# Inverse roots and two tiles' inverse sums as GpSimd powers in a linear-attention block

## The chip, the cores and the metric

One core of one Trainium2 chip. The metric is device time in microseconds of one execution of the whole program, as a median over runs.

In the profile PE is TensorE (PEld its weight loads), DVE is VectorE, ACT is ScalarE, POOL is GpSimd, and SP is the engine that issues nearly all DMAs. Each engine works through its own queue in order; a semaphore wait holds the instruction that has it and everything behind it on that engine.

## The reference

The block has 2048 tokens of width 576, 32 heads of 18 features, and an MLP of width 4608. Cut to what matters:

```python
mod = silu(c) @ w_mod                        # sa, ca, ga, sb, cb, gb
h = layernorm(x) * (1 + ca) + sa             # norm 1, 1 / sqrt(var + eps)
q, k, v = split(h @ wqkv)
phi_q = concat(softmax(q @ w_phi), softmax(-q @ w_phi))
phi_k = concat(softmax(k @ w_phi), softmax(-k @ w_phi))
kv  = phi_k^T v ;  z = sum_s phi_k
o   = (phi_q kv) / (phi_q z + 1e-6)
x   = x + ga * (o @ wo)
h   = layernorm(x) * (1 + cb) + sb           # norm 2
x   = x + gb * (relu(h @ w1) @ w2)
```

## The kernel before

**Tiles and stages.** The tokens are 16 tiles of 128 (a token on each partition). A first stage, written out by hand in the string ORDER (line 45), prepares weights and makes K, V and Q of all tiles; it ends with the first two tiles' attention and second norm. Then come eight blocks of two tiles each: first MLP layer (`l1`, or `l1_seven`), second layer (`l2`), and between them the attention and second norm of the tiles to come.

**What sets the order.** The schedule is manual. Each word of ORDER is a job of the table JOBS (line 667); jobs are issued in that order, and each engine's queue holds its instructions in the order of issue. So a job put on GpSimd stands in GpSimd's queue at the place its word has in ORDER.

**The jobs around the change**, for tile t:

- `bn` t: VectorE's mean and variance of a tile, into `mv`.
- `sa` t (`stats_a`, line 642), for tiles t and t+1 at once, on 128x2 elements: Ln of variance + eps on ScalarE into `lnv`, then Exp with scale -0.5 into `rs` (the inverse root) and Exp with scale 0.5 into a column of `sc` (the root).
- `sp` t (`stats_p`, line 647), on GpSimd: copies the mean into `sc`, a difference, and the negated inverse root into `rs`.
- `T` t: TensorE turns `sc` of two tiles (L637); `Tc` copies the rows to the input of the projections, on ScalarE (L640).
- `K` t, `V` t, `Q` t: projections on TensorE (L295). `eK` and `eQ`: two Exps on ScalarE (L300), scaled by `rs` and by its negative, which give both softmaxes' numerators.
- `sK` t: VectorE sums the 64 groups of 18 (L305) into `Rk`.
- `rK` t (`k_r`, line 320): Ln and Exp with scale -1 on ScalarE, 128x64 elements: the inverse sums `rk`.
- `pA` t (`k_scale`, L654): GpSimd makes the factors of V. `vE` t: VectorE scales V with them (L326).
- `pM` t (`k_minus`, L658, L659, L312): GpSimd copies, makes a ratio of 32 columns and multiplies half of E, 128x576, by it.
- `kv` t: nine matmuls on TensorE (L345) that add the tile's share of kv and z. They read E after `pM` and V after `vE`.
- `qs`, `qp`, `qt`: the same for Q, with a reciprocal on VectorE (L364), GpSimd's L367 and L312, and a turning DMA.
- `wo` c: GpSimd multiplies five parts of wo by ga (L692); `W` reads them (L432).

The part of ORDER where the last tiles of K run reads:

```python
kv9 rK11 K12:0 eK12 w2a1 pM10 pA11 pM11 vE10 K13:2 qs2 sK12 kv10 T14:1 eK13 V11:0 vE11 rK12 Q4:2 sK13 kv11 wo0
Tc14 V12:1 K14:0 pA12 vE12 K15:1 rK13 qs3 pM12 kv12 qp2 eQ4 qt1 eK14 sK14 sq4 gbr pA13 pM13 V13:2 vE13 eK15 Q5:0
sK15 kv13 rK14 pA14 V14:2 pM14 rK15 pA15 pM15 qt2 V15:1 vE14 kv14 Q6:2 qp3 vE15 kv15 eQ5 sq5 Q7:1 kz tp0 eQ6 eQ7
```

**Norm 2.** `ln2_rs` (line 442) does for one tile (128x1 elements) what `stats_a` does for two, without the root: Ln (L443) and Exp (L444) on ScalarE into `rs2`. `ln2_apply` (L449) on VectorE normalises with it into `xn`, which a DMA turns (in the first block TensorE, L591). `norm2` runs both for a tile; in the blocks it is called from hooks between the matmul groups.

GpSimd also adds halves of the MLP weights in the second block (L500) and does the last two operations of `fin` (L878, L879), the output of the second layer.

Of the kernel before, what the change touches and what calls it, by code (L numbers as in the profile page):

```python
# [7 lines left out]
P = 128  # L8
BF16 = mybir.dt.bfloat16
FP32 = mybir.dt.float32  # L10
FP16 = mybir.dt.float16
EPS = 1e-5
ACT = mybir.ActivationFunctionType
ALU = mybir.AluOpType
AXX = mybir.AxisListType.X

S, D, H, DH, DFF = 2048, 576, 32, 18, 4608
# [5 lines left out]
X0 = 96  # L23
# [58 lines left out]
def tile_block(ctx, tc, a, out):  # L82
# [7 lines left out]
    def small(shape, dtype, name):  # L90
        return mem.tile(shape, dtype, name=name, tag=name)

    def carve(reg, start, shape):
        n = 1
        for d in shape:
            n *= d
        names = "abcd"[:len(shape)]
        v = reg[:, start:start + n]
        return v.rearrange(f"p ({' '.join(names)}) -> p {' '.join(names)}", **dict(zip(names, shape)))
# [35 lines left out]
    sc = carve(early, 2160, (4, NX))  # L135
# [14 lines left out]
    sg = small([P, 3, NC], FP32, "sg")  # L150
    ca1 = small([P, NC], FP32, "ca1")
    mod2 = small([P, 2, 2, NC], FP32, "mod2")
    eps_t = small([P, 1], FP32, "eps_t")
    st = small([P, 4, 2, 6], FP32, "st")
    mv = small([P, 2, NT, 2], FP32, "mv")
    lnv = small([P, NT], FP32, "lnv")
    rs = small([P, NT, 2], FP32, "rs")
    rs2 = small([P, NT, 2], FP32, "rs2")
# [20 lines left out]
    act, dve, pool, sp, pe = nc.scalar, nc.vector, nc.gpsimd, nc.sync, nc.tensor  # L179
# [60 lines left out]
    load(sp, mask, "mask")  # L240

    pool.memset(zero, 0.0)
    pool.memset(eps_t[:], EPS)
    pool.tensor_copy(mk[:], ident[:, P:P + 1])
    pool.memset(m98[:], 0.0)
    pool.memset(sc, 0.0)
# [57 lines left out]
    def sums(E, Rr):  # L304
        dve.tensor_reduce(out=Rr, in_=E.rearrange("p (c e) -> p c e", e=DH), axis=AXX, op=ALU.add)  # L305
# [11 lines left out]
    def k_sums(t):  # L317
        sums(E_sb[:, t % NE, :], Rk[:, t % 4, :])

    def k_r(t):  # L320
        Rr, r = Rk[:, t % 4, :], rk[:, t % 4, :]
        act.activation(out=r, in_=Rr, func=ACT.Ln)
        act.activation(out=r, in_=r, func=ACT.Exp, scale=-1.0)

    def v_e(t, pr):
        dve.tensor_tensor(out=vv(t)[:, :, 0:DH].rearrange("p (b h) e -> p b h e", b=2),  # L326
# [113 lines left out]
        dve.tensor_tensor(out=x, in0=x, in1=pr[:, :, 0:HD], op=ALU.add)  # L440

    def ln2_rs(t):
        act.activation(out=lnv[:, t:t + 1], in_=mv[:, 1, t:t + 1, 1], func=ACT.Ln, bias=eps_t[:], scale=1.0)  # L443
        act.activation(out=rs2[:, t, 0:1], in_=lnv[:, t:t + 1], func=ACT.Exp, scale=-0.5)  # L444

    def ln2_apply(t):

# [192 lines left out]
        act.activation(out=xt_rows(t, 2), in_=bf(pr[:, 0, :])[X0:NX, 0:2 * P], func=ACT.Copy)  # L640

    def stats_a(t):
        act.activation(out=lnv[:, t:t + 2], in_=mv[:, 0, t:t + 2, 1], func=ACT.Ln, bias=eps_t[:], scale=1.0)
        act.activation(out=rs[:, t:t + 2, 0], in_=lnv[:, t:t + 2], func=ACT.Exp, scale=-0.5)
        act.activation(out=sc[:, t % 4:t % 4 + 2, X0 + 3], in_=lnv[:, t:t + 2], func=ACT.Exp, scale=0.5)

    def stats_p(t):
        c = sc[:, t % 4:t % 4 + 2, :]
# [7 lines left out]
    def k_minus(t):  # L656
# [20 lines left out]
        "rp": lambda: pool.tensor_copy(rep[0:R], siluc[0:R, :].unsqueeze(2).to_broadcast([R, NC, 32])),  # L677
        "xd": lambda t: x_scale(t, dve), "xp": lambda t: x_scale(t, pool), "xa": lambda t: x_scale(t, act),
        "bn": lambda t: bn(0, t), "sa": stats_a, "sp": stats_p,
        "T": lambda t: t_cols(t, at["T", t]), "Tc": lambda t: rows_copy(t, at["T", t]),  # L680
        "K": lambda t: proj(at["K", t], t, wk), "eK": lambda t: exps(t, at["K", t], E_sb[:, t % NE, :]),
        "Ka": lambda t: proj(at["Ka", t], t, wk, range(4)), "Kb": lambda t: proj(at["Ka", t], t, wk, [4]),
        "eKa": lambda t: exps(t, at["Ka", t], E_sb[:, t % NE, :]),
        "sK": k_sums, "rK": k_r, "pA": k_scale, "pM": k_minus,
        "V": lambda t: proj(at["V", t], t, wv), "vE": lambda t: v_e(t, at["V", t]), "kv": kv_job,
        "FQ": lambda c: fold_chunk(c, at["FQ", c]),
# [9 lines left out]
        "ot": lambda i: turn(o_sb[:, i, :], at["ot", i]),  # L696
        "oc": lambda i: act.activation(out=flat(oT[:, i]), in_=bf(at["ot", i][:, 0, :])[:, 0:640], func=ACT.Copy),
        "W": lambda i: wo_mm(i, at["W", i]), "xr": lambda i: add_res(i, at["W", i]), "lb": lambda i: bn(1, i), "lr": ln2_rs,
        "ap": lambda i: ln2_apply(i),
        "ht": lambda i: turn2(xn[:, i, :], at["ht", i]),  # L700
# [277 lines left out]
    def norm2(t):  # L978
        ln2_rs(t)
        ln2_apply(t)  # L980
        i = t % 2
        turn_dma(h2[:, t // 2 % 2, :, i * P:(i + 1) * P], xn[:, i, :])
# [96 lines left out]
    def in_seven(b):  # L1079
        t = 2 * b + 2  # L1080

        def hook(k):
            if b + 1 == NB:
                if k in (2, 4, 6):
                    scale_b22(k // 2 - 1)
                return
            if k < 2:
                add_res(t + k, WO[k])
            elif k < 4:
                bn(1, t + k - 2)  # L1090
            elif k < 6:
                ln2_rs(t + k - 4)
            else:
                ln2_apply(t + k - 6)
                i = k - 6
                turn_dma(h2[:, (b + 1) % 2, :, i * P:(i + 1) * P], xn[:, i, :])
        return hook
# [125 lines left out]
```

## Time and profile before

| | |
|---|---|
| median of 3 runs | 376.39 us (376.04 to 376.88) |
| span of the profiled execution, first to last instruction | 374.9 us |
| granted TensorE clock | 0.999 |
| VectorE, ScalarE busy | 282.2 us, 220.8 us |
| Ln and Exp of `stats_a` (L643 to L645), 8 of each | 287, 204 and 194 ns |
| Ln and Exp of `k_r` (L322, L323), 16 of each | 257 and 256 ns |
| Ln and Exp of `ln2_rs` (L443, L444), 16 of each | 294 and 203 ns |
| GpSimd 128x2: L649, L650, L651 | 187, 210, 228 ns |
| GpSimd 128x32: L659, L654 | 266, 364 ns |
| GpSimd 128x576: L312 | 1166 to 1182 ns |

The profiled execution has a span alone; what lies around it is in the runs, whose median is 1.5 us above the span. In a row of the timeline the columns are start in us, length in us, engine, line, operation, output<-inputs with shapes, the count, and in brackets the idle time of the engine just before with what ended it. Rows of the waits are: who waited <- for what: total us, times, longest.

### The profile page before, as it was taken

To read this page: it belongs to the slowest core of one execution; us is meant where nothing else is said; L and a number is where in the kernel's file an instruction comes from. 1 tells how busy PE (TensorE), PEld (TensorE's weight loads), DVE (VectorE), ACT (ScalarE), POOL (GpSimd) and SP (SyncE) were. 2 spreads that over 40 slices of the span, in tenths; PEclk is the share of its full clock that TensorE was granted. 3 is DMA by queue.
4 is the path that set the end of the run, shared out by engine and by line. 5 is a ranking of instruction groups with operands and counts; after the bars stand their busy time and mean duration, and the time that the engine had idled before them with its cause. 6 is when DMAs were issued, how large, how long until landed. Compare 5 with 4: busy or idle time off the path is not lost.

```text
span 374.9 us, 14287 instructions
## 1 busy us (share of the span) xinstructions
PE 368.7 (98%) x6245; PEld 314.7 (84%) x6245; DVE 282.2 (75%) x506; ACT 220.8 (59%) x497; POOL 139.7 (37%) x202
## 2 busy tenths in 40 slices
PE   7999999999999999999999999999999999999996
PEld 3778788888887788889988987998799889979975
DVE  3899998788979779987795778678678647745742
ACT  1799997679533435608752782477178518744820
POOL 2178899850302567380053007102600240044023
PEclk9999999999999999999999999999999999999999
DMA  7996699978966437473227216530523023101001
GB/s 293 414 422 259 213 425 247 292 191 310 177 168 129 126 80 155 122 148 78 36 52 175 41 29 83 146 68 20 128 52 37 20 49 35 37 0 36 3 2 33
DMA packets 58593, 49.96 MB, mean 133 GB/s; under 512 B 46881, under 2 KB 50850, under 8 KB 57762
## 3 DMA queue, kind: packets, MB, share of 16 engines
q1 hardware_dynamic: 58242, 48.85, 48.7%
q8 instruction: 49, 0.80, 0.9%
q10 hardware_dynamic: 288, 0.19, 0.2%
q14 instruction: 14, 0.11, 0.1%
HBM read 31.98 MB, written 5.90 MB: 101 GB/s over the span
## 4 chain that ended last, share of the span: by engine, by line
PE 88%; DMA 4%; ACT 3%; DVE 2%; issue 1%; SPq 0%; DVEq 0%
PE PS L890 33%; PE PS L810 23%; PE PS L295 10%; PE PS L744 10%; PE PS L958 4%; PE PS L793 3%; DMA x_sb<-in_xk_dram 2%; ACT RT L300 2%; DMA R<-in_wkT_dram 2%; PE PS L415 2%; PE PS L345 1%; DVE early L305 1%; PE PS L965 1%; PE PS L432 1%; PE PS L930 1%; DVE st L256 1%
## 5 line engine op out<-in xcount | busy, mean ns | idle before, releaser
L890 PEld LDWEIGHTS <-RH 128*128 128x128 f16 x846 | 81.7, 98 | 21.2 <-issue 0.4
L878 POOL TENSOR_TENSOR yt<-yt,gb_row 128x288 f32<-128x288 f32 x23 | 27.5, 1194 | 177.3 <-DVE yt L877 177.3
L810 PEld LDWEIGHTS <-R 64*128 64x128 bf16 (+1 forms) x1824 | 76.5, 94 | 0.8 <-issue 0.6
L890 PE MATMUL PS<-R,RH 128*128 128x288 bf16 (+1 forms) x558 | 73.2, 286 | 0.0
L810 PE MATMUL PS<-h,R 64*128 64x128 bf16 x1056 | 58.6, 216 | 0.0
L840 ACT ACTIVATE RH<-PS 128x512 f16<-128x512 f32 x96 | 51.9, 602 | 7.4 <-PE PS L810 7.0
L300 ACT ACTIVATE RT<-PS,rs 128x576 bf16<-128x576 f32 x64 | 42.8, 745 | 2.3 <-PE PS L295 1.8
L810 PE MATMUL PS<-RE,R 64*128 64x128 f16 x768 | 38.7, 216 | 0.1
L890 PE MATMUL PS<-RT,RH 128*128 128x288 f16 x288 | 37.9, 286 | 0.0
L744 PE MATMUL PS<-h,R 64*128 64x256 bf16 (+1 forms) x684 | 36.1, 264 | 0.0
L744 PEld LDWEIGHTS <-R 64*128 64x128 bf16 x684 | 31.6, 94 | 3.9 <-issue 0.2
L295 PE MATMUL PS<-RH,R 116*128 116x288 bf16 x240 | 32.5, 286 | 0.1
L987 ACT ACTIVATE h<-h,mod 128x256 bf16<-128x256 bf16 x63 | 32.4, 589 | 0.0
L295 PE MATMUL PS<-RH,RT 116*128 116x288 bf16 x240 | 31.9, 286 | 0.2 <-ACT RT L300 0.2
L830 ACT ACTIVATE yt<-PS 128x512 f32<-128x512 f32 x10 | 6.0, 597 | 43.4 <-PE PS L810 43.4
L810 PEld LDWEIGHTS <-w 64*128 64x128 f16 (+1 forms) x480 | 29.0, 94 | 0.0
L894 ACT ACTIVATE RS<-PS 128x288 f32<-128x288 f32 x24 | 9.8, 410 | 32.2 <-PE PS L890 32.2
L256 DVE BATCH_NORM_STATS2 st<-x_sb 128x6 f32<-128x288 bf16 x64 | 25.6, 442 | 3.4 <-DMA x_sb<-in_xk_dram 3.4
L877 DVE TENSOR_TENSOR yt<-PS,RS 128x288 f32<-128x288 f32 x23 | 10.5, 456 | 23.4 <-PE PS L890 23.3
L295 PEld LDWEIGHTS <-R 116*128 116x128 bf16 x240 | 22.7, 98 | 6.1 <-issue 0.5
L295 PEld LDWEIGHTS <-RT 116*128 116x128 bf16 x240 | 22.9, 98 | 5.8 <-issue 0.3
L879 POOL TENSOR_TENSOR x_sb<-yt,x_sb 128x288 bf16<-128x288 f32 x30 | 24.9, 833 | 3.6 <-DVE yt L875 1.8
(152 smaller groups left out, 753.9 us busy)
## 6 DMA issues: line engine op xcount, KB each, us to landing
R<-in_w_dram SPq DMA_DIRECT2D x4, 1152.0 KB, 8.6
eqd<-RT SPq DMA_DIRECT2D x12, 288.0 KB, 2.1
RT<-eqd SPq DMA_DIRECT2D x12, 288.0 KB, 3.3
R<-in_w2b_dram SPq DMA_DIRECT2D x2, 1296.0 KB, 8.7
R<-in_w2a_dram SPq DMA_DIRECT2D x3, 864.0 KB
out_dram<-x_sb SPq DMA_DIRECT2D x15, 144.0 KB, 2.1
RT<-in_xT_dram SPq DMA_DIRECT2D x2, 640.0 KB
x_sb<-in_xk_dram SPq DMA_DIRECT2D x8, 144.0 KB, 2.7
```

The source lines that it names most:

```text
L256: dve.bn_stats(out=s[:, hf, :], in_=x_sb[:, t % 8 if n else t, hf * HD:(hf + 1) * HD])
L295: pe.matmul(pr[:, k, 0:HD], lhsT=xt(t, ck), rhs=w[0:R, ck, k * HD:(k + 1) * HD], start=(ck == 0), stop=(ck == NC - 1))
L300: act.activation(out=E.rearrange("p (b h s e) -> p b h s e", b=2, s=2, e=DH)[:, :, :, s, :], in_=pr[:, :, 0:HD].rearrange("p b (h e) -> p ...
L744: pe.matmul(PS[:, 2 * u + hf, n * 256 + o:n * 256 + o + w], lhsT=w1_lhs(hf, c, j, h), rhs=hb[b0:b0 + 64, c, o:o + w], start=(n == 0 and c ...
L793: pe.matmul(PS[:, bank_at[n], j * 256:j * 256 + 256], lhsT=w1_lhs(hi, c, j, hi), rhs=hb[64 * hi:64 * hi + 64, c, :], start=(j == 0 and c = ...
L810: pe.matmul(PS[:, bank_at[BK[n] + str(g)], i * P:(i + 1) * P], lhsT=w[r, (4 * c + i) * P:(4 * c + i + 1) * P], rhs=x, start=(n in ("M1", " ...
L840: act.activation(out=o, in_=v[{"k11": "Y", "k12": "Z", "k21": "X", "k22": "W"}[n]], func=ACT.Relu)
L878: pool.tensor_tensor(out=y, in0=y, in1=gb_row[:, c], op=ALU.mult)
L879: eng.tensor_tensor(out=xs(t)[:, c], in0=y, in1=xs(t)[:, c], op=ALU.add)
L890: pe.matmul(PS[:, bank, 0:HD], lhsT=am[:, j, :], rhs=bm[:, j, :], start=first and j == 0, stop=(j % 9 == 8), skip_group_check=True)
L958: pe.matmul(pr[:, k, 0:HD], lhsT=oT[:, t % 2, ci, :], rhs=wo_sb[:, ci, k * HD:(k + 1) * HD], start=(ci == 0), stop=False, skip_group_check ...
L987: act.activation(out=o, in_=o, func=ACT.Identity, scale=mod(1, c), bias=mod(0, c))
```

## The change

ScalarE's Ln and Exp are replaced by GpSimd's tensor_tensor with the operation pow, whose second operand is a column of constants, -0.5 or -1, read with a stride of 0. `stats_a` becomes an add of eps, a power and a product (root = value times inverse root), `ln2_rs` an add and a power, all on GpSimd. `k_r` becomes one power for tiles 14 and 15 and stays as it was for tiles 0 to 13. The tile of eps is gone; a tile of the two exponents is there, with one more memset. ORDER is unchanged.

```diff
-    eps_t = small([P, 1], FP32, "eps_t")
+    pw = small([P, 2], FP32, "pw")
...
-    pool.memset(eps_t[:], EPS)
+    pool.memset(pw[:, 0:1], -0.5)
+    pool.memset(pw[:, 1:2], -1.0)
...
+    def power(o, i, k, shape):
+        pool.tensor_tensor(out=o, in0=i, in1=pw[:, k:k + 1].to_broadcast(shape), op=ALU.pow)
+
     def k_r(t):
         Rr, r = Rk[:, t % 4, :], rk[:, t % 4, :]
-        act.activation(out=r, in_=Rr, func=ACT.Ln)
-        act.activation(out=r, in_=r, func=ACT.Exp, scale=-1.0)
+        if t < 14:
+            act.activation(out=r, in_=Rr, func=ACT.Ln)
+            act.activation(out=r, in_=r, func=ACT.Exp, scale=-1.0)
+        else:
+            power(r, Rr, 1, [P, 2 * H])
...
     def ln2_rs(t):
-        act.activation(out=lnv[:, t:t + 1], in_=mv[:, 1, t:t + 1, 1], func=ACT.Ln, bias=eps_t[:], scale=1.0)
-        act.activation(out=rs2[:, t, 0:1], in_=lnv[:, t:t + 1], func=ACT.Exp, scale=-0.5)
+        pool.tensor_scalar(out=lnv[:, t:t + 1], in0=mv[:, 1, t:t + 1, 1], scalar1=EPS, scalar2=None, op0=ALU.add)
+        pool.tensor_tensor(out=rs2[:, t, 0:1], in0=lnv[:, t:t + 1], in1=pw[:, 0:1], op=ALU.pow)
...
     def stats_a(t):
-        act.activation(out=lnv[:, t:t + 2], in_=mv[:, 0, t:t + 2, 1], func=ACT.Ln, bias=eps_t[:], scale=1.0)
-        act.activation(out=rs[:, t:t + 2, 0], in_=lnv[:, t:t + 2], func=ACT.Exp, scale=-0.5)
-        act.activation(out=sc[:, t % 4:t % 4 + 2, X0 + 3], in_=lnv[:, t:t + 2], func=ACT.Exp, scale=0.5)
+        pool.tensor_scalar(out=lnv[:, t:t + 2], in0=mv[:, 0, t:t + 2, 1], scalar1=EPS, scalar2=None, op0=ALU.add)
+        power(rs[:, t:t + 2, 0], lnv[:, t:t + 2], 0, [P, 2])
+        pool.tensor_tensor(out=sc[:, t % 4:t % 4 + 2, X0 + 3], in0=lnv[:, t:t + 2], in1=rs[:, t:t + 2, 0], op=ALU.mult)
```

GpSimd's queue has 59 instructions more (one of them a memset), ScalarE's 60 fewer. The powers of tiles 14 and 15 stand in GpSimd's queue directly ahead of `pA14` and `pA15`.

## The prediction

> **What bounds the kernel now.** I read first the page's busy shares, then the waits of PE, then busy time by stage.
>
> ```profile
> PE 368.7 (98%) x6245; PEld 314.7 (84%) x6245; DVE 282.2 (75%) x506; ACT 220.8 (59%) x497; POOL 139.7 (37%) x202
> PE PS L251 <- POOL eps_t L243: 1.3, 1, 1.3
> PE PS L464 <- DMA R<-in_wkT_dram: 0.8, 1, 0.8
> PE PS L280 <- ACT RT L300: 0.3, 1, 0.3
> PE PS L289 <- DVE RS L673: 0.2, 1, 0.2
> PE PS L295 <- ACT RT L300: 0.2, 1, 0.2
> 37.00:56.00 19.00, 18.84 (x205) 15.17 (x203) 17.86 (x33) 18.37 (x46) 16.88 (x34) 1.00 0.80 310
> 56.00:76.00 20.00, 20.00 (x210) 16.42 (x208) 16.32 (x19) 13.74 (x33) 17.25 (x35) 1.00 1.06 261
> ```
>
> PE is the bound. Of its 6.2 us of idle time the five waits hold 2.8; the rest lies after its last matmul. Only two of them, 0.3 and 0.2 us, wait for ScalarE, so relief of ScalarE is worth at most 0.5 us. The last two rows are stages (length, then busy PE, PEld, DVE, ACT, POOL). In the K/V stage POOL is no idle engine: 16.88 of 19 us and 17.25 of 20, where its share of the whole span is 37%. So the question is what the added GpSimd work makes late, and who waits for it. The timelines of POOL and of PE tell:
>
> ```profile
> 50.14 1.16 POOL L312 TENSOR_TENSOR RT<-RT,early 128x576 bf16<-128x576 bf16 x1
> ...
> 53.22 0.19 POOL L649 CAST early<-mv 128x4 bf16<-128x4 f32 x1
> 53.48 0.20 POOL L650 TENSOR_TENSOR early<-mv,early 128x2 bf16<-128x2 f32 x1
> 53.65 0.23 POOL L651 TENSOR_SCALAR rs<-rs 128x2 f32<-128x2 f32 x1
> 53.85 0.36 POOL L654 TENSOR_SCALAR early<-early,rs 128x32 f32<-128x32 f32 x1
> ...
> 56.14 1.17 POOL L312 TENSOR_TENSOR RT<-RT,early 128x576 bf16<-128x576 bf16 x1
> 57.89 0.36 POOL L654 TENSOR_SCALAR early<-early,rs 128x32 f32<-128x32 f32 x1 [0.59 <-DVE RT L326]
> ...
> 59.33 1.17 POOL L312 TENSOR_TENSOR RT<-RT,early 128x576 bf16<-128x576 bf16 x1
> ...
> 70.26 0.36 POOL L654 TENSOR_SCALAR early<-early,rs 128x32 f32<-128x32 f32 x1 [1.18 <-ACT early L323]
> 71.08 1.17 POOL L312 TENSOR_TENSOR RT<-RT,early 128x576 bf16<-128x576 bf16 x1
> 72.44 0.36 POOL L654 TENSOR_SCALAR early<-early,rs 128x32 f32<-128x32 f32 x1 [0.20 <-ACT early L323]
> 73.26 1.17 POOL L312 TENSOR_TENSOR RT<-RT,early 128x576 bf16<-128x576 bf16 x1
> ```
>
> ```profile
> 58.10 0.51 PE L345 MATMUL PS<-RT 128*128 128x76 bf16 x9
> 60.90 0.51 PE L345 MATMUL PS<-RT 128*128 128x76 bf16 x9
> 73.45 0.51 PE L345 MATMUL PS<-RT 128*128 128x76 bf16 x9
> 75.03 0.51 PE L345 MATMUL PS<-RT 128*128 128x76 bf16 x9
> ```
>
> The L312 rows are job pM of tiles 7, 9, 10, 14 and 15: the product on E that releases job kv of that tile, nine matmuls of L345 on PE. The four PE rows are kv9, kv10, kv14 and kv15. POOL has no idle row between 44.03 and 57.31.
>
> **Step 1: what a statistics pair costs on POOL.** stats_a of two tiles puts an add, a power and a product ahead of the three operations of stats_p, and pM and pA of the next tiles stand behind them. Starts in the rows above: an operation that reads the one before starts 0.07 after its end (L649 ends 53.41, L650 starts 53.48), an independent one 0.17 after the start (L650 to L651). Add as L651: 0.23 + 0.07 = 0.30. Power: a + 0.07. Product: 0.17. Sum 0.54 + a.
>
> **Step 2: the power.** The trace has none. Below: it can't be cheaper than a plain TENSOR_TENSOR, 210 ns at 128x2 (L650) and 266 ns at 128x32 (L659), so 1.8 ns a column over some 206 ns; 0.33 us at 64 columns. Above: a power is a logarithm, a product and an exponential. If GpSimd makes them in software, as chains of such plain passes, I put them at up to 50 passes: 90 ns a column, so 0.39 us at 128x2 and 6 us at 128x64. My value, an estimate: sixteen passes (seven for the logarithm, one product, eight for the exponential), 30 ns a column. So a = 0.27 at 128x2 and b = 2.13 at 128x64; a pair costs 0.81.
>
> **Step 3: pairs 0 to 8** (before 44 us). T needs what stats_p writes. T0 starts on PE at 11.76; POOL had ended L650 at 9.73 and is 0.8 later; covered, with 1.2 us left. The later ones go into POOL's idle time: 3.11 us ahead of its 19.33, 1.01 at 27.98, 0.93 at 33.79, 1.41 at 44.03. Cost 0, under 0.1 where kv4 (39.17) has 0.8 us behind pM4 (ends 38.34). Without that idle time each would cost up to 0.8.
>
> **Step 4: pairs 10, 12 and 14.** No idle time is left ahead of them but 0.59 us at 57.89.
> - kv7 starts at 52.03, pM7 ends at 51.30; 0.81 later it is 0.1 late.
> - kv9: pM9 ends at 57.31 and two pairs make it 58.93; PE could start at 58.10. +0.9 (the 0.2 us that PE regains from ScalarE at 55.62 is a gap within this; it moves nothing).
> - kv10: the 0.59 of idle time, a wait for DVE's L326 at 57.87, goes first. POOL is 1.62 - 0.59 = 1.03 late, pair 14 makes it 1.8. pM10 ends 60.50 + 1.8 = 62.3 and kv10 starts there, not at 60.90: +1.4 in all, with the 0.9 inside.
>
> PE's stream is dense after this, so nothing gives the 1.4 back; kv11 to kv13 have over 1.3 us behind their products and follow.
>
> **Step 5: the sums of tiles 14 and 15.** Ln and Exp (256 ns each) leave ScalarE; the power waits on POOL for DVE's sum. Before, sum 14 ended at 69.58 and pA14 started at 70.26, 0.68 later; now 0.07 + 2.13 + 0.07 = 2.27 later: 1.59 more. pM14 ended 72.25, 1.2 ahead of kv14; that slack pays, 0.45 is left: PE +1.9. Power 15 stands behind pM14 in the queue, though its sum is ready: pM14 ends 72.25 + 1.4 + 1.6 = 75.3, power to 77.4, pA15 at 77.5 against 72.44, so pM15 ends 79.5 and kv15 starts there, not at 75.03: **+4.4 in all**. Behind it on POOL stand qp3 and three wo products (80.41), 1.2 us ahead of L432 at 81.62: just covered. Each further 1 us of b costs 2 us, once for each tile; below b = 0.6 step 5 costs nothing.
>
> **Step 6: norm 2.** Sixteen times L443 and L444 (294 + 203 ns) become an add and a power, 0.30 + 0.24 us plus 0.07. Hidden: POOL waits 177.3 us for DVE ahead of L878 in these stages, and its result is needed a block later. In the second block it stands behind L500 (1352 ns), eight of them; DVE's L449 waits there, and matmuls of L890 behind it. I take 0 from between -0.2 (ScalarE's queue ahead of L449 at 88.31 is gone) and +0.5.
>
> **Step 7: ScalarE** loses 8 x 0.69 + 16 x 0.50 + 4 x 0.26 = 14.5 us of busy time, worth nothing but the gaps of L280 and L295: inside the above.
>
> [...] The first tensor operation on POOL (L650, 9.53) took 0.20 us: no load shows. [...]
>
> **Sum.** 374.9 + 4.4 = 379.3 us of span. The runs shown have a median of 376.39, 1.5 over the span; I put the same on: **380.8 us**, slower by 1.2%.
>
> **The rivals.**
> - *Cheap power* (under 12 ns a column, b under 1): a pair costs 0.75, steps 4 and 5 come to 0.8 at kv9 and 1.3 at kv10, tiles 14 and 15 add 0 to 0.7: 377.6 to 378.4. For it: the plain rows. Against: no other POOL row does more than one pass. 0.22.
> - *Dear power* (over 60 ns, b over 4): 4.4 + 2 x 1.9 and 3 x 0.06 for the pairs, 385 and up; at 90 ns 389. For it: software, column by column. Against: nothing that the trace shows. 0.28.
> - *The first power waits for its code*: the nearest load in the trace is ScalarE's table, 1.28 us (L177), which T0's 1.2 us cover but for 0.1. It decides only above 1.2 us; with a load of five such rows PE stands 5.2 us at T0: 386. Against: L650 at 9.53. 0.03.
> - *Not slower: ScalarE sets the pace and POOL has room.* The chain of waits runs on ScalarE from 42.83 to 55.62, and POOL is idle for 63% of the span. Then the gaps of 0.3 and 0.2 close, 375.9. It decides if two pairs fit into kv9's 0.79 us, that is under 0.39 us a pair; but add and product alone make 0.47 without the power. 0.09.
>
> Forecast (12 to 60 ns a column, 378.4 to 385): 0.38.
>
> **Range and chances.** Low 377.0, below the cheap power's bound and above the not slower case (0.09 out); high 390, a power of 95 ns a column (about 0.1 out). 0.2% is 0.75 us, about what a measurement tells from no change. Faster by more needs more than PE's 0.5 us of gaps: 0.02. Within 0.2%: the rest of the not slower case, and a little of the cheap one: 0.09. Slower: 0.89.
>
> **What would show it.** Right: POOL rows of the power near 0.27 and 2.1 us; waits of L345 on POOL's L312 at kv9, kv10, kv14 and kv15; span up by those waits; PE's busy time unchanged. Wrong: no PE wait on POOL (the not slower case); a hole at the first power; powers as long as L650 (cheap). If PE's waits on L312 stay under 0.5 us the queue argument of steps 4 and 5 is wrong; if they are there with another size, only step 2 is.

## The result, and the profile after

The changed kernel takes **405.56 us** (median of 4 runs, 404.61 to 406.87), against 376.60 us for the kernel before on the same chip: a ratio of 1.0775 (95% interval 1.0752 to 1.0798). It is 29 us slower, where 4.4 had been forecast, and it lies above the range. The span of the profiled execution is 403.4 us, 28.5 more than before.

Lines move down by 7 in most places: L345, the matmuls of `kv`, is now L352; GpSimd's product on E, L312, is L313; PE's projections, L295, are L296; `pA`, L654, is L661; `T`, L637, is L644. In the new code L322 is the power of `k_r` and `stats_a`, L451 that of `ln2_rs`.

First the busy shares (the page's first part) and the waits of PE (who waits <- for what: total us, times, longest):

```profile
PE 374.2 (93%) x6245; PEld 316.4 (78%) x6245; DVE 282.5 (70%) x506; ACT 211.6 (52%) x437; POOL 181.7 (45%) x261
PE PS L352 <- POOL RT L313: 21.5, 6, 9.4
...
PE PS L897 <- DVE RH L761: 0.9, 1, 0.9
...
PE PS L281 <- ACT RT L301: 0.3, 1, 0.3
```

A line that was not there before now leads the table: `kv` waits 21.5 us for GpSimd's product on E. ScalarE has 9 us less to do, and the gap of 0.3 us that PE spends waiting for it stands where it stood; the one of 0.2 us is gone. The 0.9 us of L897 (before L890, matmuls of the MLP's second layer) are what norm 2 costs (experiment 6). Now what GpSimd is busy with, in groups of instructions with shapes kept apart (count | busy us, mean ns of one | idle time before):

```profile
L322 POOL TENSOR_TENSOR early<-early,pw 128x64 f32<-128x64 f32 x2 | 21.1, 10549 | 0.3 <-DVE early L306 0.3
L451 POOL TENSOR_TENSOR rs<-lnv,pw 128x1 f32<-128x1 f32 x16 | 9.0, 563 | 1.3
L322 POOL TENSOR_TENSOR rs<-lnv,pw 128x2 f32<-128x2 f32 x8 | 5.8, 729 | 0.7
```

The three shapes lie on a line of 0.40 us + 0.158 us a column: 0.56, 0.72 and 10.5 us. A power of 64 columns lasts 10.55 us, five times the 2.13 of the prediction. The timeline of GpSimd (start, length) shows the two in their places:

```profile
73.39 1.17 POOL L313 TENSOR_TENSOR RT<-RT,early 128x576 bf16<-128x576 bf16 x1
74.86 10.55 POOL L322 TENSOR_TENSOR early<-early,pw 128x64 f32<-128x64 f32 x1 [0.30 <-DVE early L306]
85.51 0.37 POOL L661 TENSOR_SCALAR early<-early,rs 128x32 f32<-128x32 f32 x1
...
86.34 1.17 POOL L313 TENSOR_TENSOR RT<-RT,early 128x576 bf16<-128x576 bf16 x1
87.47 10.55 POOL L322 TENSOR_TENSOR early<-early,pw 128x64 f32<-128x64 f32 x1
...
98.94 1.16 POOL L313 TENSOR_TENSOR RT<-RT,early 128x576 bf16<-128x576 bf16 x1
```

and the timeline of PE shows who waits for them:

```profile
61.94 0.52 PE L352 MATMUL PS<-RT 128*128 128x76 bf16 x9 [0.99 <-POOL RT L313]
66.02 0.52 PE L352 MATMUL PS<-RT 128*128 128x76 bf16 x9 [1.11 <-POOL RT L313]
...
76.13 2.62 PE L296 MATMUL PS<-RH,RT 116*128 116x288 bf16 x20
87.57 0.82 PE L352 MATMUL PS<-RT 128*128 128x76 bf16 x9 [8.82 <-POOL RT L313]
88.19 2.60 PE L296 MATMUL PS<-RH,R 116*128 116x288 bf16 x10
100.16 0.82 PE L352 MATMUL PS<-RT 128*128 128x76 bf16 x9 [9.37 <-POOL RT L313]
100.79 2.60 PE L296 MATMUL PS<-RH,R 116*128 116x288 bf16 x10
```

The four are kv9, kv10, kv14 and kv15. Power 14, pM14, power 15 and pM15 follow each other on GpSimd (with `pA` between) without a pause; each kv starts just after its pM (86.34 + 1.17 is 87.51; 98.94 + 1.16 is 100.10). Between them PE does ten matmuls and has nothing else. Those ten take 2.60 us instead of 1.39, since the granted clock is down. Windows of the span show it (length, then busy PE, PEld, DVE, ACT, POOL; the third number from the end is the granted clock):

```profile
80.00:81.00 1.00, 0.00 (x0) 0.00 (x0) 0.00 (x0) 0.00 (x0) 1.00 (x1) 1.00 0.00 0
81.00:81.50 0.50, 0.00 (x0) 0.00 (x0) 0.00 (x0) 0.00 (x0) 0.50 (x1) 0.64 0.00 0
...
88.00:100.00 12.00, 2.79 (x16) 1.54 (x13) 0.76 (x1) 1.38 (x2) 11.82 (x5) 0.50 0.06 25
...
104.50:105.00 0.50, 0.50 (x4) 0.32 (x3) 0.00 (x0) 0.30 (x1) 0.50 (x2) 0.50 0.00 0
105.00:106.00 1.00, 1.00 (x23) 0.88 (x22) 0.10 (x1) 0.48 (x1) 1.00 (x1) 0.98 0.35 134
```

PE's last matmul before the wait ends at 78.75 (76.13 + 2.62). The clock falls to half at 81.1 (the 0.64 is the mean of a window that holds both), 2.4 us later, and is back at 105.0, 4.9 us after kv15 begins.

**Where the time went**, by the starts of the same matmuls in the two timelines of PE:

| matmul | before, us | after, us | later by |
|---|---|---|---|
| kv1 | 27.82 | 28.79 | 1.0 |
| kv4 | 39.17 | 41.36 | 2.2 |
| T12 | 55.18 | 58.17 | 3.0 |
| kv9 | 58.10 | 61.94 | 3.8 |
| kv10 | 60.90 | 66.02 | 5.1 |
| kv14 | 73.45 | 87.57 | 14.1 |
| kv15 | 75.03 | 100.16 | 25.1 |
| the `W` matmuls (L432, now L439) | 81.62 | 109.09 | 27.5 |
| second block | 151.59 | 180.11 | 28.5 |
| last matmuls | 369.36 | 398.04 | 28.7 |

kv1 before stands inside a row of 18 matmuls; its 27.82 is worked out from that row. So the pairs of statistics up to kv10 cost 5.1 us (0.2 of them PE was late already at kv0, behind a DMA at the start), the sums of tiles 14 and 15 another 20.0, the slow clock behind kv15 2.4, and norm 2, in the second block, 1.0: 28.5 in all.

### The profile page after: what moved, and what is told of

It reads as the page before. It is cut to its first block, busy times and chain, and to the rows that moved or that the text cites. A ratio compares the mean times of both kernels' runs of the same rounds, so it can differ in the third digit from the quotient of the medians.

```text
span 403.4 us, 14310 instructions
## 1 busy us (share of the span) xinstructions
PE 374.2 (93%) x6245; PEld 316.4 (78%) x6245; DVE 282.5 (70%) x506; ACT 211.6 (52%) x437; POOL 181.7 (45%) x261
## 4 chain that ended last, share of the span: by engine, by line
PE 70%; POOL 19%; DMA 4%; DVE 3%; issue 2%; ACT 0%; SPq 0%; POOLq 0%; DVEq 0%
PE PS L897 30%; PE PS L817 21%; POOL early L322 5%; POOL RT L313 5%; PE PS L296 4%; PE PS L751 4%; PE PS L800 3%; PE PS L965 3%; DMA x_sb<-in_xk_dram 2%; POOL w L507 2%; DMA R<-in_wkT_dram 2%; PE PS L422 1%; POOL rs L322 1%; POOL early L661 1%; DVE early L306 1%
## 5 line engine op out<-in xcount | busy, mean ns | idle before, releaser
L897 PEld LDWEIGHTS <-RH 128*128 128x128 f16 x846 | 81.8, 98 | 22.3 <-issue 1.5
L897 PE MATMUL PS<-R,RH 128*128 128x288 bf16 (+1 forms) x558 | 73.2, 286 | 0.9 <-DVE RH L761 0.9
L897 PE MATMUL PS<-RT,RH 128*128 128x288 f16 x288 | 37.9, 286 | 0.0
L296 PE MATMUL PS<-RH,R 116*128 116x288 bf16 x240 | 34.7, 299 | 0.0
L296 PE MATMUL PS<-RH,RT 116*128 116x288 bf16 x240 | 32.8, 291 | 0.0
L333 DVE TENSOR_TENSOR RT<-PS,early 128x576 bf16<-128x576 f32 x16 | 11.9, 751 | 25.4 <-POOL early L661 22.1
L296 PEld LDWEIGHTS <-R 116*128 116x128 bf16 x240 | 23.7, 102 | 6.8 <-issue 0.2
L352 PE MATMUL PS<-RT 128*128 128x76 bf16 (+1 forms) x144 | 8.9, 210 | 21.5 <-POOL RT L313 21.5
L296 PEld LDWEIGHTS <-RT 116*128 116x128 bf16 x240 | 23.3, 100 | 6.1
L884 DVE TENSOR_TENSOR yt<-PS,RS 128x288 f32<-128x288 f32 x23 | 10.5, 456 | 23.0 <-PE PS L897 22.9
```

The source lines that it names most:

```text
L296: pe.matmul(pr[:, k, 0:HD], lhsT=xt(t, ck), rhs=w[0:R, ck, k * HD:(k + 1) * HD], start=(ck == 0), stop=(ck == NC - 1))
L897: pe.matmul(PS[:, bank, 0:HD], lhsT=am[:, j, :], rhs=bm[:, j, :], start=first and j == 0, stop=(j % 9 == 8), skip_group_check=True)
```

## The experiments

The theory after this result: the mechanism of steps 4 and 5 holds (queue, then PE), and the price of a power, far above the bound put on it, accounts for the size. Rivals: the queue itself, whatever stands in it, costs most; the two groups of powers only hurt together; the stride of 0 or a first use makes the powers slow; taking ScalarE's work away brings a gain that the stall hides. Experiments 1 to 4 ran on a chip where the kernel before took 377.01 us, 5 to 8 where it took 376.72.

**1. The roots alone.** All inverse sums go back to ScalarE.

```diff
-        if t < 14:
+        if t < 16:
             act.activation(out=r, in_=Rr, func=ACT.Ln)
```

> The changed kernel with the inverse sums of tiles 14 and 15 back on ScalarE; both norms' roots stay on GpSimd. Theory price (a power on GpSimd costs about 0.40 us and 0.16 us a column, and stands in an in-order queue that kv waits for): the two 64-column powers made about 20 us of TensorE's waits and the slow clock behind them 2.4 us, so this kernel is at 376.6 + 5.1 (pairs) + 1.0 (norm 2) = 382.7 us, between 381.5 and 383.5, and the waits of 9 us are gone. Rival spread (the loss is of the norm's powers as much as of the sums): 390 us or more.

Measured: 382.95 us, ratio 1.0157 (1.0140 to 1.0173), a loss of 5.9. The waits of `kv` are down to 3.3 us, the longest 1.1; the two of 9 us are gone.

**2. The sums alone.** Both norms' roots go back to ScalarE.

```diff
     def ln2_rs(t):
-        pool.tensor_scalar(out=lnv[:, t:t + 1], ...)
-        pool.tensor_tensor(out=rs2[:, t, 0:1], ..., op=ALU.pow)
+        act.activation(out=lnv[:, t:t + 1], ..., func=ACT.Ln, bias=eps_t[:], scale=1.0)
+        act.activation(out=rs2[:, t, 0:1], ..., func=ACT.Exp, scale=-0.5)
...
     def stats_a(t):
-        pool.tensor_scalar(...)
-        power(rs[:, t:t + 2, 0], lnv[:, t:t + 2], 0, [P, 2])
-        pool.tensor_tensor(...)
+        act.activation(..., func=ACT.Ln, bias=eps_t[:], scale=1.0)
+        act.activation(..., func=ACT.Exp, scale=-0.5)
+        act.activation(..., func=ACT.Exp, scale=0.5)
```

> The changed kernel with both norms' roots back on ScalarE; only the inverse sums of tiles 14 and 15 are powers on GpSimd. Theory price: 376.6 + about 20 (two waits of kv, each the 10.5 us of a power less its slack) + 2.4 (the clock behind them) = 399 us, between 397.5 and 400.5; with the kernel that has only the roots the losses add up to the whole 29 us within 1 us. Rival interplay (POOL is late already when it reaches the sums, and that makes them so dear): the two losses add up to 25 us or less.

Measured: 398.96 us, ratio 1.0585 (1.0560 to 1.0611), a loss of 22.0. In its waits of PE `kv` (here L354) keeps the two long ones:

```profile
PE PS L354 <- POOL RT L315: 18.2, 2, 9.4
```

The two losses add up to 27.9 us, against 29.0 for the whole change. The 1.1 us between them is a little more than the 1 us expected, but less than the intervals of the three ratios leave open (some 1.4 us, an estimate). As far as these runs can tell, the groups cost together what they cost alone; the rival that they only hurt together falls.

**3. Plain products in the powers' places.** The same 59 instructions on GpSimd in the same order, but cheap.

```diff
-        ... op=ALU.pow)
+        ... op=ALU.mult)
```

> The changed kernel with a plain product in the place of every power, same shapes, same queues, same waits; the inverse roots and the two tiles' inverse sums are so not computed. Theory price: what is left is the queue at the price of a plain operation, which the forecast had worked out as 1.1 to 1.3 us of waits at kv9 and kv10: 377.5 to 378.2 us. Rival queue (the added instructions and their waits on POOL make the loss, whatever they compute): 390 us or more. Rival clock: no long wait, so granted clock 0.99 or more under both.

Measured: 379.35 us, ratio 1.0066 (1.0044 to 1.0089). The rows of the products are 292 ns (128x64), 195 (128x2) and 189 (128x1). So the price of the powers makes all but 2.3 of the 29 us, and the queue as such does not. But the 2.3 is some twice the 1.1 to 1.3 us expected, and the time lies above the expected 378.2: kv4 is 0.6 us late, kv9 1.6, kv10 2.4. The waits of PE in this kernel:

```profile
PE PS L352 <- POOL RT L313: 1.6, 2, 1.0
```

The timeline of GpSimd shows where the rest comes from, in pair 12 of this kernel:

```profile
53.47 1.17 POOL L313 TENSOR_TENSOR RT<-RT,early 128x576 bf16<-128x576 bf16 x1
54.73 0.22 POOL L650 TENSOR_SCALAR lnv<-mv 128x2 f32<-128x2 f32 x1
55.03 0.20 POOL L322 TENSOR_TENSOR rs<-lnv,pw 128x2 f32<-128x2 f32 x1
...
55.71 0.20 POOL L657 TENSOR_TENSOR early<-mv,early 128x2 bf16<-128x2 f32 x1
56.01 0.23 POOL L658 TENSOR_SCALAR rs<-rs 128x2 f32<-128x2 f32 x1
56.21 0.36 POOL L661 TENSOR_SCALAR early<-early,rs 128x32 f32<-128x32 f32 x1
```

In the kernel before, the product on E ahead of the same pair is

```profile
52.11 1.16 POOL L312 TENSOR_TENSOR RT<-RT,early 128x576 bf16<-128x576 bf16 x1
```

From the start of the product on E to `pA` (L661) are 2.74 us. Before it was 1.74 (52.11 to 53.85), so a pair costs 1.00 more, of which 0.20 are the power's stand-in: 0.80 for the rest, where step 1 has 0.54. The pair's first operation starts 1.26 after the start of the product ahead of it (53.47 to 54.73), where the old one did after 1.11 (52.11 to 53.22), and L658 starts 0.30 after L657 (55.71 to 56.01), where the same two stood 0.17 apart before. What makes these two gaps longer was not tried.

**4. PE kept busy in the waits.** In the changed kernel, dummy matmuls (job `Y`, the function that already fills a wait at the start) stand ahead of kv14 and kv15, and `eQ5` is issued earlier to make room for them.

```diff
-... V15:1 vE14 kv14 Q6:2 qp3 vE15 kv15 eQ5 sq5 Q7:1 ...
+... V15:1 eQ5 vE14 Y30 kv14 Q6:2 qp3 vE15 Y44 kv15 sq5 Q7:1 ...
...
+        "Y": lambda i: spin(i, 0),
```

> The changed kernel with 30 and 44 dummy matmuls of 512 columns in a free bank ahead of kv14 and kv15, where TensorE would stand idle for 9 us each (and the Exps of tile 5's Q issued ahead of them, so that the bank is free). Theory clock: the granted clock of 0.5 behind the two waits costs 2.4 us after kv15, so this kernel is 2 to 2.5 us faster than the changed one, near 403.2 us, and the Q projections behind kv15 take 1.2 us for ten again instead of 2.6. Rival: the slow clock there is hidden by other waits or comes anyway, and the time stays at 405.6 us.

Measured: 403.19 us, ratio 1.0697 (1.0676 to 1.0718); the interval of the changed kernel, 1.0752 to 1.0798, lies above it. kv15 still starts at 100.07. Windows of this kernel, columns as above:

```profile
77.00:88.00 11.00, 8.64 (x55) 4.50 (x53) 0.76 (x1) 0.25 (x1) 10.82 (x6) 1.00 0.15 44
88.00:101.00 13.00, 11.64 (x68) 5.85 (x67) 1.29 (x3) 1.37 (x2) 12.74 (x7) 1.00 0.07 24
101.00:112.00 11.00, 11.00 (x111) 9.03 (x110) 9.07 (x16) 8.01 (x13) 5.88 (x6) 1.00 0.64 193
```

The clock stays at 1.00 all through, the ten matmuls of L296 behind kv15 take 1.39 us again, and from kv15 to `W` are 6.6 us (100.07 to 106.67), as before the change, and not 8.9. By the medians 2.4 us come back, by the ratios 2.9. That is the share of the slow clock, as the table of matmuls has it (2.4).

**5 and 6. Norm 1 alone, norm 2 alone.** Experiment 1 with `ln2_rs`, or with `stats_a`, put back on ScalarE as in experiment 2.

> The kernel before with only the first norm's roots as GpSimd powers (eight pairs). Theory price: the kernel with both norms' roots lost 5.9 us in its ratio; 5.1 us of that stood in its trace by kv10, so 5.1 us remain here, 381.5 to 382.5. Rival: the second norm's sixteen powers hold half of it, and this kernel is at 380 or less.

> The kernel before with only the second norm's roots as GpSimd powers (sixteen of one column). Theory price: 0.5 to 1.1 us slower (377.5 to 378.1 with 377.0 for the kernel before), all of it in the second block, where the powers stand behind GpSimd's weight sums; the later blocks hide theirs. Rival of the forecast's step 6: no loss, within 0.3 us of the kernel before.

Measured: norm 1 alone 381.95 us, ratio 1.0135 (1.0114 to 1.0156); norm 2 alone 378.40 us, ratio 1.0040 (1.0023 to 1.0057), a loss of 1.5 (0.9 to 2.1) and so a little more than expected. The place is the one that step 6 names, in the second block. The waits of PE, the timeline of VectorE and that of GpSimd in the kernel with norm 2 alone (VectorE's `ln2_apply`, before L449, is L458 here; GpSimd's weight halves, before L500, are L509):

```profile
PE PS L899 <- DVE RH L763: 0.9, 1, 0.9
```

```profile
144.82 1.05 DVE L458 TENSOR_SCALAR xn<-x_sb,mv,rs 128x576 bf16<-128x576 bf16 x2 [2.17 <-POOL rs L453]
...
148.20 1.05 DVE L458 TENSOR_SCALAR xn<-x_sb,mv,rs 128x576 bf16<-128x576 bf16 x2 [0.76 <-POOL rs L453]
```

```profile
142.78 1.17 POOL L315 TENSOR_TENSOR RT<-RT,ratq 128x576 bf16<-128x576 bf16 x1
143.92 0.22 POOL L452 TENSOR_SCALAR lnv<-mv 128x1 f32<-128x1 f32 x1
144.22 0.57 POOL L453 TENSOR_TENSOR rs<-lnv,pw 128x1 f32<-128x1 f32 x1
144.76 2.27 POOL L509 TENSOR_TENSOR w<-w,x_sb 128x512 f16<-128x512 bf16 x2
146.99 0.52 POOL L452 TENSOR_SCALAR lnv<-mv 128x1 f32<-128x1 f32 x1
147.60 0.56 POOL L453 TENSOR_TENSOR rs<-lnv,pw 128x1 f32<-128x1 f32 x1
```

The first tile's add and power stand behind the product for Q (L315), and VectorE waits 2.17 us for them at L458. The second tile's stand behind two weight halves, and VectorE waits another 0.76 us. The work behind them on VectorE (L763) is late, and PE waits 0.9 us for that. The changed kernel has the same two waits of VectorE (2.17 and 0.76 us).

**7. The price by itself.** The kernel before, with eleven operations on a scratch tile put into GpSimd's queue in the second layers of blocks 2 to 6.

```diff
+    def price(n, op, full=False):
+        e = pb[:, 0:n] if full else pb[:, 0:1].to_broadcast([P, n])
+        pool.tensor_tensor(out=pa[:, 0:n], in0=pa[:, 0:n], in1=e, op=op)
```

> The kernel before with eleven added GpSimd operations on a scratch tile in the second layers of blocks 2 to 6, where GpSimd waits for VectorE: powers of 1, 2, 4, 8, 16, 32, 48 and 64 columns with the exponent read with a stride of 0, one power of 48 columns with a full tile of exponents, and plain products of 48 columns in both forms. Theory price, per column: 0.40 us and 0.159 us a column: 0.56, 0.72, 1.04, 1.67, 2.94, 5.5, 8.0, 10.6 us, the same 8.0 with a full tile, and 0.30 for the products. Rival stride: the repeated exponent is what is slow, and the full tile takes under half. Rival first use: the price is that of rare or cold code, and later powers are shorter than the first. Time of the whole: within 0.3 us of the kernel before plus what its longest powers make late there, at most 2 us.

The timeline of GpSimd in this kernel (the last two rows are products, the two powers of 48 columns read the exponent with a stride of 0 and from a full tile):

```profile
203.09 2.90 POOL L1054 TENSOR_TENSOR pa<-pa,pb 128x16 f32<-128x16 f32 x1
231.61 5.60 POOL L1054 TENSOR_TENSOR pa<-pa,pb 128x32 f32<-128x32 f32 x1
240.86 8.01 POOL L1054 TENSOR_TENSOR pa<-pa,pb 128x48 f32<-128x48 f32 x1
268.92 8.20 POOL L1054 TENSOR_TENSOR pa<-pa,pb 128x48 f32<-128x48 f32 x1
280.76 10.53 POOL L1054 TENSOR_TENSOR pa<-pa,pb 128x64 f32<-128x64 f32 x1
305.55 0.45 POOL L1054 TENSOR_TENSOR pa<-pa,pb 128x48 f32<-128x48 f32 x1
315.91 0.29 POOL L1054 TENSOR_TENSOR pa<-pa,pb 128x48 f32<-128x48 f32 x1
```

The price grows with the columns, about 0.16 us for each (the power of 4 columns, 1.19 us, lies 0.16 above the line; the exponents tried are -0.5 and -1). The full tile is no cheaper (8.20 against 8.01 us), which ends the rival of the stride; a product of the same 48 columns takes 0.29 to 0.45 us. The time of this kernel missed its expectation: 385.69 us, ratio 1.0232 (1.0203 to 1.0260), a loss of 9.0 where at most 2.3 had been expected. Its waits of PE name the place, the second layer's sums, and VectorE's timeline names GpSimd behind it:

```profile
PE PS L814 <- DVE yt L881: 6.0, 2, 4.3
```

```profile
238.74 0.46 DVE L881 TENSOR_TENSOR yt<-PS,RS 128x288 f32<-128x288 f32 x1 [5.19 <-POOL x_sb L883]
...
278.65 0.46 DVE L881 TENSOR_TENSOR yt<-PS,RS 128x288 f32<-128x288 f32 x1 [7.76 <-POOL x_sb L883]
```

`fin`'s last two operations (here L882 and L883) stood behind a power, VectorE's L881 waited for them, and PE for L881: 1.7 us behind the power of 32 columns, 4.3 behind that of 48 with the full tile. The mean granted clock is 0.996 over the span of 383.5 us, which can cost PE some 1.5 us more (an estimate, 0.4% of that span); the rest of the 9.0 was not followed. These stages have GpSimd idle most of the time (in the kernel before it is busy for 79.7 of the 264 us from 108 to 372), and yet a long operation in its queue reaches PE.

**8. What the change could bring at most.** The kernel before, with no roots and no inverse sums of tiles 14 and 15 at all.

```diff
     def ln2_rs(t):
-        act.activation(...)
-        act.activation(...)
+        pass
...
     def stats_a(t):
-        act.activation(...)
-        act.activation(...)
-        act.activation(...)
+        pass
...
     def k_r(t):
-        act.activation(...)
-        act.activation(...)
+        if t < 14:
+            act.activation(...)
+            act.activation(...)
```

> The kernel before without the ScalarE work that the change takes away, and with nothing put on GpSimd in its place: both norms' inverse roots are constants, and the inverse sums of tiles 14 and 15 are those of tiles 10 and 11. It gives the most that the change could have gained. Theory: TensorE's stream is dense, and only the two waits for ScalarE of 0.3 and 0.2 us go: 0.2 to 0.6 us faster, 376.4 to 376.8 with 377.0 for the kernel before. Rival relief: ScalarE's queue sets the pace of the K/V stage, as the chain of waits says, and 14.5 us less on it are worth 2 us or more.

Measured: 376.86 us, ratio 1.0004 (0.9990 to 1.0018): no gain, where 0.2 to 0.6 us had been expected. The span is 374.9 us, as before. PE's 0.3 us wait for ScalarE is still in its table; the 0.2 is gone, and kv15 starts 0.36 us earlier (74.67 against 75.03), of which 0.10 is left at the last matmuls (369.26 against 369.36). So there is nothing behind the stall: a power that cost nothing would not have made this kernel faster by an amount that these runs can tell.

## Why the prediction was wrong

**The place was right, the price was not.** The waits of L345 on L312 (now L352 on L313) at kv9, kv10, kv14 and kv15 are all there; the prediction said that if they came with another size, step 2 was at fault. It is:

| term | predicted | measured |
|---|---|---|
| step 2, power of 128x64 | 2.13 us | 10.55 us |
| step 2, power of 128x2 | 0.27 us | 0.73 us |
| step 1, pair without its power | 0.54 us | 0.81 us |
| steps 3 and 4, PE late at kv10 | 1.4 us | 5.1 us |
| step 5, tiles 14 and 15 | 3.0 us (4.4 less 1.4) | 20.0 us |
| step 6, norm 2 | 0 | 1.0 us (1.5 alone) |
| slow clock | not in the sum | 2.4 us |
| sum | 4.4 us | 28.5 us |

- **Step 2 is the step that failed.** Its bounds were worked out from plain passes, 1.8 ns a column at the low end and 50 passes, 90 ns, at the high end. The chip shows 158 ns, 88 of those passes, on a fixed part of 0.40 us. No row before bore on the number of passes, neither on the sixteen nor on the 50; the 50 was a guess that was then used as a bound, and the range ended near it. The two powers of 64 columns alone carry 17 of the 24 us between forecast and result (20.0 less 3.0).
- **Step 5** stands as a mechanism. Its rule that each further 1 us of a power costs 2 gives 2 x (10.55 - 2.13) = 16.8 on top of 3.0, that is 19.8; measured 20.0.
- **Step 1** was 0.27 short. It took its start-to-start times from the old order; in the new one two gaps are longer, by 0.15 and 0.13 us (experiment 3). With the power, a pair costs 0.81 + 0.73 = 1.54 and not 0.81.
- **Step 3** gave the early pairs' cost as nothing, with up to 0.8 us each if the cover went. At 1.54 the cover is too small (the step itself read 0.8 us of it at kv4): kv1 is 1.0 late, kv4 2.2, T12 3.0. Two waits of `T` for `stats_p` (0.7 us in all) are among them; the step looked at T0 alone. Experiment 3, at 1.00 a pair, loses only 0.6 by kv4.
- **Step 4** stands, with the entry that step 3 leaves: kv9 and kv10 wait 0.99 and 1.11 us.
- **Step 6** named the place, the order behind the weight halves and the engine that waits; it did not name the product for Q, behind which the first tile's power stands. Its upper bound of 0.5 was too low: 1.0 in the whole change, 1.5 alone. Why it is more alone than in the sum was not tried, and the interval of 0.9 to 2.1 holds both.
- **The slow clock** was no term of the prediction. The longest wait that it worked out for PE was 2.5 us (4.4 less 1.9, at kv15); in experiment 4 a wait of 2.35 us leaves the clock at 1.00.
- **Step 7** holds: experiment 8 takes more from ScalarE than the change does, and gains nothing. ScalarE does not set the pace. In the changed kernel the rows of ScalarE's groups add up to 221.5 us instead of 235.4, near the 14.5 less of the step; its busy share falls by 9.2 alone, as rows that overlap count once.
- **The rivals.** The dear power is what happened, in kind; the 60 to 90 ns a column that were worked out for it were still too low. The cheap power and the case in which ScalarE sets the pace fall. So does the one in which the first power waits for its code. The rows of GpSimd in the changed kernel:

```profile
9.71 0.24 POOL L650 TENSOR_SCALAR lnv<-mv 128x2 f32<-128x2 f32 x1 [3.65 <-DVE mv L258]
10.03 0.73 POOL L322 TENSOR_TENSOR rs<-lnv,pw 128x2 f32<-128x2 f32 x1
10.85 0.20 POOL L652 TENSOR_TENSOR early<-lnv,rs 128x2 bf16<-128x2 f32 x1
```

The first power takes 0.73 us like the seven later ones (0.73 to 0.74), and no hole stands beside it: it starts 0.08 us after the end of the add ahead of it, and the product behind it starts 0.09 us after its own end.

PE's busy time was to stay the same and rose by 5.5 us, to 374.2; three groups of ten matmuls of L296 at half clock (2.60, 2.60 and 2.31 us instead of 1.39) account for 3.3 of it, kv14 and kv15 (0.82 instead of 0.51) for 0.6; the rest was not followed.

## What to carry to other kernels

An operation that no trace shows has no upper bound from the rows of other operations: measure it at two sizes in a scratch run before it goes into a queue, or leave the range open upwards. A share of idle time (GpSimd, 63% of the span) is not room, because a long operation delays whatever stands behind it in the queue: in experiment 7 a power of 8.20 us made VectorE wait 7.76 and PE 4.3 us. And before moving work off an engine, leave that work out once: where, as in experiment 8, the time does not fall, there is nothing for a move to gain.

## What was not expected of the hardware

- **GpSimd's power costs 0.40 us + 0.158 us a column** of 128 partitions in f32, close to a line from 1 to 64 columns: 8.0 us at 48 columns where a product takes 0.3 to 0.45, and 10.55 us at 64 where ScalarE's Ln and Exp together took 0.51. What inside it takes the time stays open.
- **The two waits of PE of 8.82 and 9.37 us cost more than the waits.** In the changed kernel the granted clock fell from 1.00 to 0.50 2.4 us after the last matmul and came back 4.9 us after kv15 began (81.14 to 105.04); 2.4 us were lost by it, and dummy matmuls got them back (experiment 4). The 4.9 us are no constant. In experiment 2, where PE waits 8.77 and 9.39 us, kv14 and kv15 take 0.82 us each and the ten matmuls behind kv15 2.60, as in the changed kernel; but the next ten take 1.58 us, where the changed kernel has 2.31, so the clock came back sooner. After shorter waits `kv` takes 0.52 us: after 0.99 and 1.11 us in the changed kernel, and after 2.35 us in experiment 4, with the clock at 1.00. How long a wait may last, and how much work keeps the clock up, no run here shows.
